# An attention unit's softmax steps re-staged inside the paired MoE blocks

## The chip, the cores and the metric

The kernel runs on one core of a Trainium2 chip. The metric is device time in microseconds (us) of one execution. Its engines are called here as the profile calls them: PE (TensorE, matrix products; PEld is its weight load), DVE (VectorE), ACT (ScalarE), POOL (GpSimd) and SP (SyncE, which here only issues DMAs). Each engine works through its own instructions in the order in which they were written; they wait for each other by semaphores.

## The reference, cut to what is computed

Chunked attention over 64 tokens, then a layer with a hard gate (h times a ramp clipped to 0..1), then a second layer with a softmax, a normalisation and a product. The change touches the attention and the first layer alone.

```python
scores = scale * np.matmul(q_c, k_c.transpose(0, 1, 2, 4, 3))
scores = scores - np.max(scores, axis=-1, keepdims=True)
attn = np.exp(scores)
attn = attn / (np.sum(attn, axis=-1, keepdims=True) + 1e-09)
out = np.matmul(attn, v_c)
...
h = x @ w_in
relu6 = np.clip(h + 3.0, 0.0, 6.0)
g = h * relu6 / 6.0
return (g @ w_out).astype(np.float32)
```

8 heads, 4608 tokens, x of 512, w_in 512x2048, w_out 2048x512, all fp32.

## The kernel before

The 4608 tokens are 36 attention units `u` of 128 tokens and 9 blocks of 512. Blocks 0 to 2 run one at a time, with the attention between their products. Blocks 3 to 8 run as three pairs. Pairs 0 and 1 are `pair_7` (310 to 491 us and 491 to 674 us of the trace); pair 2 is another function, `pair`. The order of all instructions is written out by hand: the scheduler takes them as the code issues them.

A pair computes the two blocks' first layer with seven half-size products in place of eight. **First half** of a pair: eight steps `j` (256 of the 2048 hidden columns each; their results are four quarters, two token blocks by two halves). A step on PE is seven calls of `mul7`, each six matmuls of 128x512 on one PSUM bank: A11 (into bank `a`), S2 (`b`), S1 (`c`), then A22 and S4 *of the step before*, whose banks come in `late` (the function `finish`), then S3 (added to `b`) and A12 (added to `a`). DVE and ACT make four sums of them and gate each: `a` (gated by `gate`, L1230, after a ramp on ACT, L1225), `u3 + c` (L1369, L1371: the quarter `c22`, gated by two ramps on ACT, L1225 and L1227, and a product on POOL, L1374), `s1 + b` after A22 (L1301) and `u2 + c` after S4 (L1305). Four POOL subtractions (`later_sums`, L1318 to L1321) make further operands, and SP stores them. A22 adds to the bank that L1369 has to read first, and S3 to the bank that L1345 has to read first.

In the steps j = 1, 2, 3, 4, 6, 7 an **attention slot** (`att_slot`) stands at the step's end: on PE the scores of unit u+2 and the product of unit u with v, each 32 matmuls of 64x64 (L398). Between them a unit goes through: row maxima (DVE, L410), their scaling by -0.125 (DVE, L431), eight exponentials with sums (ACT, L448), 1/sum (DVE, L454 and L457), the multiplication with it (`attn_norm`, L465; POOL in the first half, DVE in the second), five 32x32-block transposes (`attn_turn`; DVE, L490 and L494), the product with v, and two copies of its result (ACT, L520). In a slot's step of unit u the code issues `attn_norm(u)` and the exponentials of u+1 behind A11, and `attn_turn(u)` behind `finish`. The maxima of u+2 also wait for the two ACT copies, which read the same PSUM tile.

**Second half**: seven products of eight steps (`mul_o`, L1280), whose operands `prepare(d)` splits into a high and a low part (ACT cast L1264, DVE subtraction L1265). `prepare(0)` and `prepare(1)` stand in the last step of the first half, `prepare(2)` behind the last `finish`; the products j = 0, 2, 4, 6 of the second half begin with the operands 0, 1, 2, 3. Two slots stand behind j = 7 of the first and the second product ("slot 0" and "slot 1" below). In pair 1 no unit is left for their scores.

Of the kernel before, what the change touches and what calls it, by code (L numbers as in the profile page):

```python
# [21 lines left out]
def tile_kernel(  # L22
# [404 lines left out]
    def attn_scores_act(u, sc, between=None):  # L427
        mx = maxima(sc)
        if between:
            between()  # L430
        nc.vector.tensor_scalar_mul(out=mx, in0=mx, scalar1=-0.125)  # L431
        exps[u] = sc, mx
# [560 lines left out]
    def att_slot(w, u, coming=None):  # L993
        t = att_psum()
        sc = None
        if u < NU:
            sc = scores(u, t)
        if w is not None:
            if w >= FIRST * UPB:
                attn_pv_raw(w, t, raw_dest(w))  # L1000
            else:
                attn_pv(w, t, *xn[w // UPB])
            p_t.pop(w, None)
        loads = [lambda eng: load_v(w + 2, eng=eng)] if w is not None else []
        if u < NU:
            loads.append(lambda eng: load_qk(u + 1, eng=eng))
        if coming is None:
            for load in loads:
                load(nc.scalar)
        else:  # L1010
            coming.extend(loads)
        if u < NU:
            attn_scores_act(u, sc)

    def raw_dest(w):

# [186 lines left out]
    def o_next():  # L1203
        if pend:
            moe_o(*pend.pop(0))
# [17 lines left out]
    def ramp(h, t, down=False):  # L1223
        s = -1.0 / 6.0 if down else 1.0 / 6.0
        nc.scalar.activation(out=t, in_=h, func=AF.Relu, bias=half_1, scale=s)  # L1225
        if down:
            nc.scalar.activation(out=t, in_=t, func=AF.Relu, bias=one_1, scale=-1.0)  # L1227
# [62 lines left out]
    def pair_7(p, todo):  # L1290
# [5 lines left out]
            while coming:  # L1296
                coming.pop(0)(nc.sync)

        def finish(j, b, c, s1, u2):
            mul7(b, j, "A22", "T4", False, True)  # L1300
            nc.vector.tensor_add(out=b, in0=s1, in1=b)  # L1301
            t = gp_tile("t")
            ramp(b, t)
            mul7(c, j, "S4", "B22", False, True)
            nc.vector.tensor_add(out=c, in0=u2, in1=c)  # L1305
            gate(t, b, g_t["B21", j // 2][:, j % 2])
            t = gp_tile("g_hi")
            ramp(c, t)
            while waiting:
                waiting.pop(0)()  # L1310
            return j, t, c

        def later_sums(j, g12):
# [8 lines left out]
            for i, t in enumerate((t2, t3, t4)):  # L1322
                waiting.append(
                    lambda i=i, t=t: nc.sync.dma_start(out=later_t[i, m][:, k], in_=t)
                )

        event = {1: 0, 2: 1, 3: 2, 4: 3, 6: 4, 7: 5}
        for j in range(NJ):
            u = base + event[j] if j in event else NU
            n = 2 * (j % 2)  # L1330
            a = acc_bank(n) if j else att_psum()[:, 0]
            mul7(a, j, "A11", "B11", True, False)
            s1 = work_tile("s")
            nc.scalar.copy(out=s1, in_=a)
            load_coming()
            while todo:
                todo.pop(0)()
            if base < u < NU:
                attn_norm(u, nc.gpsimd)
                if u + 1 < NU:  # L1340
                    attn_exp_act(u + 1, range(H))
            b = acc_bank(n + 1) if j else h_psum()
            mul7(b, j, "S2", "T2", True, False)
            u2 = work_tile("s")
            nc.vector.tensor_add(out=u2, in0=s1, in1=b)  # L1345
            if j % 2 == 0:
                for g in GROUPS:
                    g_t[g, j // 2] = home(g, j // 2)
            m, k = j // 2, j % 2
            if j == 1:  # L1350
                made = finish(*late)
                mul7(b, j, "S3", "T3", False, False)
            c = h_psum()
            mul7(c, j, "S1", "T1", True, False)
            o_next()
            if j > 1:
                made = finish(*late)
            if base < u < NU:
                attn_turn(u)
            if j == NJ - 1:  # L1360
                prepare(0)
            if made:
                i, t, ps = made
                gate(t, ps, t)
                later_sums(i, t)
            if j != 1:
                mul7(b, j, "S3", "T3", False, False)
            u3 = ap1.tile([P, DM], F32, tag="tx2", name="tx2")
            nc.vector.tensor_add(out=u3, in0=s1, in1=b)  # L1369
            c22 = g_t["B22", m][:, k]  # L1370
            nc.vector.tensor_add(out=c22, in0=u3, in1=c)  # L1371
            t = gp_tile("g_lo")
            ramp(c22, t, True)
            nc.gpsimd.tensor_mul(out=c22, in0=t, in1=c22)  # L1374
            mul7(a, j, "A12", "B21", False, True)
            t = gp_tile("t")
            ramp(a, t)
            o_next()
            if j == NJ - 1:
                prepare(1)  # L1380
            gate(t, a, g_t["B11", m][:, k])
            if u < NU:
                att_slot(u, u + 2, coming)
            late = j, b, c, s1, u2
        i, t, ps = finish(*late)
        gate(t, ps, t)
        prepare(2)
        later_sums(i, t)
# [10 lines left out]
        for i in range(len(OUTS)):  # L1399
# [7 lines left out]
            for j in range(NJ):  # L1407
                mul_o(ps, i, j, i in (0, 1, 3, 6), i in (2, 4, 5, 6))
                d = (i * NJ + j) // 2
                if (i, j) == (0, 5):  # L1410
                    while waiting:
                        waiting.pop(0)()
                if j % 2:
                    bring(d)
                else:
                    prepare(d + 3)
                if (i, j) in steps:
                    todo.pop(0)()
                u = base + 6 + i
                load_coming()  # L1420
                if i < 3:
                    if j == 0 and u < NU:
                        attn_norm(u)
                        if u + 1 < NU:
                            attn_exp_act(u + 1, range(H))
                    elif j == 2 and u < NU:
                        attn_turn(u)
                    elif j == 7 and i < 2:
                        att_slot(u, u + 2, coming)
                if final:  # L1430
                    if (i, j) == (5, 7):
                        second.append(Second())
                    elif (i, j) in ((6, 4), (6, 7)):
                        second[0].window(1, 0, False)
                    if j % 2 and d % 2 == 0 and d > 2 * ND:
                        load_o(d // 2 - ND - 1)
# [198 lines left out]
    for F, n in SLOT_AT.items():  # L1635
        u = 2 * UPB + 1 + n
        STEPS.setdefault(F, []).append(("exp", u, range(H // 2)))
        STEPS.setdefault(F + 1, []).append(("exp", u, range(H // 2, H)))
        if u <= NA:
            STEPS.setdefault(F + 2, []).append(("norm", u, (0, 1, 2)))  # L1640
            STEPS.setdefault(F + 3, []).append(("turn", u, (3, 4)))
    u = 2 * UPB
# [178 lines left out]
```

## Time and profile before

| what | value |
|---|---|
| three runs | median 1222.01 us, 1218.27 to 1223.95 |
| the profiled execution | 1221.51 us, span 1219.7 us |
| busy in the span | PE 97%, PEld 79%, DVE 74%, ACT 59%, POOL 39% |
| granted PE clock, mean | 0.989 |

The span runs from the first to the last instruction; the execution takes 1.8 us more. A row of the timeline says when a group of like instructions started (us from the span's start), how long it took from the start of its first to the end of its last, and in brackets how long its engine had been idle before it and who released it. Matmuls overlap, so a PE row's end is modelled, and the distance between two starts is the better measure. A wait row says who waited for whom, for how long in total, how often, and the longest. The stretch rows give each engine's busy time in it, the granted clock (1.00 is 2.4 GHz, 0.50 is 1.2 GHz), the share of time in which DMA engines were busy, and GB/s.

### The profile page before, as it was taken

The numbers are of one execution on the slowest core, as the hardware profiler recorded it, in microseconds if no ns is written. First come the engines' busy times: TensorE is split into PE (matmuls) and PEld (weight loads), VectorE is DVE, ScalarE is ACT, GpSimd is POOL, SyncE is SP. The second block draws the span as 40 slices with busy tenths as digits, with TensorE's granted clock in tenths as the row PEclk, the third lists the DMA queues.
The fourth block names the chain that finished last, engine by engine and source line by source line (L and its number), as shares of the span: only waits on it lengthen the run. The fifth ranks groups of instructions, "written<-read, shape, count | busy, mean of one in ns | idle before, by whom it ended". The sixth has DMA issues, their size and how long they took to land.

```text
span 1219.7 us, 21402 instructions
## 1 busy us (share of the span) xinstructions
PE 1183.7 (97%) x7199; PEld 960.8 (79%) x7199; DVE 900.8 (74%) x1434; ACT 720.7 (59%) x1655; POOL 479.8 (39%) x560
## 2 busy tenths in 40 slices
PE   8999999999999899999799799999999999999998
PEld 7888877878877688777588688888888888888887
DVE  7888677776577887477867666767987887877774
ACT  7765545554445574345553343355887777777775
POOL 1000674442246400256400011200486758585864
PEclk9999999999999899999899899999999999999999
DMA  9812657765888896788799999882332323232311
GB/s 371 362 52 76 232 209 253 267 234 193 296 296 274 279 390 207 246 283 286 249 330 342 356 348 341 308 311 87 111 96 72 97 70 99 71 98 71 99 55 63
DMA packets 172254, 258.61 MB, mean 212 GB/s; under 512 B 19056, under 2 KB 86896, under 8 KB 172144
## 3 DMA queue, kind: packets, MB, share of 16 engines
q1 hardware_dynamic: 159760, 234.69, 56.5%
q10 hardware_dynamic: 12384, 22.55, 5.3%
q8 instruction: 57, 0.93, 0.3%
q14 instruction: 53, 0.43, 0.1%
HBM read 170.40 MB, written 76.02 MB: 202 GB/s over the span
## 4 chain that ended last, share of the span: by engine, by line
PE 74%; issue 8%; DVE 7%; POOL 5%; ACT 3%; DMA 2%; SPq 0%; POOLq 0%; ACTq 0%; DVEq 0%
PE po L949 16%; PE acc L574 15%; PE hp L535 8%; PE acc L1280 7%; PE b L751 5%; PE hp L1143 5%; PE hp L1280 4%; PE c L751 4%; PE a L751 4%; PE att L1143 2%; PE att L398 2%; PE att L751 1%; DVE wi L1265 1%; DVE pbd L494 1%; PE acc L1143 1%
## 5 line engine op out<-in xcount | busy, mean ns | idle before, releaser
L574 PE MATMUL acc<-g_hi,wo 128*128 128x512 f32 x640 | 164.2, 396 | 0.0
L574 PEld LDWEIGHTS acc<-g_hi,wo 128*128 128x128 f32 x640 | 119.7, 189 | 26.5
L1143 PE MATMUL hp<-wi,w 128*128 128x512 f32 x468 | 119.5, 399 | 7.4 <-ACT wi L319 6.6
L1143 PEld LDWEIGHTS hp<-wi,w 128*128 128x128 f32 x468 | 89.8, 193 | 28.9 <-issue 7.0
L1143 PE MATMUL acc<-wi,w 128*128 128x512 f32 x420 | 106.8, 401 | 3.5 <-DVE tx L1369 3.5
L864 ACT COPY wo<-wo 32x256 f32<-32x256 f32 x228 | 92.1, 404 | 19.4 <-DVE wo L846 11.5
L1280 PE MATMUL acc<-wi,w 128*128 128x512 f32 x408 | 98.0, 398 | 3.3 <-DVE wi L1265 3.0
L535 PE MATMUL hp<-x_hi,wi 128*128 128x512 f32 x384 | 97.8, 396 | 0.1
L1143 PEld LDWEIGHTS acc<-wi,w 128*128 128x128 f32 x420 | 79.3, 191 | 21.4 <-DVE tx L1369 3.8
L1280 PEld LDWEIGHTS acc<-wi,w 128*128 128x128 f32 x408 | 77.3, 191 | 21.9 <-DVE wi L1265 3.8
L732 POOL TENSOR_TENSOR x_lo<-xr,x_hi 128x768 fp32r<-128x768 f32 (+1 forms) x30 | 63.8, 2148 | 75.5 <-ACT x_hi L725 72.6
L448 ACT ACTIVATE p<-att,mx 128x64 f32<-128x64 f32 x256 | 76.5, 322 | 26.5 <-DVE mx L431 18.2
L1265 DVE TENSOR_TENSOR wi<-wo,wi 128x1024 fp32r<-128x1024 f32 x50 | 66.0, 1336 | 32.8 <-ACT wi L1264 32.3
L574 PE MATMUL acc<-g_lo,wo 128*128 128x512 f32 x320 | 87.8, 390 | 0.0
L535 PEld LDWEIGHTS hp<-x_hi,wi 128*128 128x128 f32 x384 | 71.5, 187 | 17.1 <-ACT x_hi L512 0.3
L1264 ACT CAST wi<-wo 128x1024 fp32r<-128x1024 f32 x50 | 51.7, 1070 | 35.8 <-PE hp L1280 19.0
L574 PEld LDWEIGHTS acc<-g_lo,wo 128*128 128x128 f32 x320 | 60.4, 189 | 13.0
L836 DVE SCALAR_TENSOR_TENSOR wo<-wo,r,wo 128x1024 f32<-128x1024 f32 x36 | 68.9, 1913 | 1.3
L933 POOL TENSOR_TENSOR wo<-wo,wo 128x1024 fp32r<-128x1024 f32 x25 | 64.5, 2578 | 6.2 <-ACT wo L929 3.6
L560 POOL TENSOR_TENSOR g_lo<-t,g_hi 128x512 fp32r<-128x512 f32 x15 | 21.5, 1433 | 106.4 <-ACT g_hi L557 106.4
L1454 POOL TENSOR_TENSOR s<-s 128x512 f32<-128x512 f32 x4 | 5.1, 1300 | 130.2 <-DVE s L1453 130.2
L448 ACT ACTIVATION_READ_ACCUMULATOR p<-att,mx 128x1 f32 x256 | 55.0, 215 | 0.0
(318 smaller groups left out, 2873.6 us busy)
## 6 DMA issues: line engine op xcount, KB each, us to landing
w<-sti SPq DMA_DIRECT2D x168, 256.0 KB, 4.7
w<-sto SPq DMA_DIRECT2D x112, 256.0 KB, 4.8
later_t<-xo SPq DMA_DIRECT2D x48, 256.0 KB, 4.7
wo<-later_t SPq DMA_DIRECT2D x24, 512.0 KB, 6.2
wo<-wo SPq DMA_DIRECT2D x328, 32.0 KB, 1.8
x2d<-xo SPq DMA_DIRECT2D x36, 256.0 KB, 4.3
xr<-x2d SPq DMA_DIRECT2D x36, 256.0 KB, 3.3
out<-ob SPq DMA_DIRECT2D x36, 256.0 KB, 2.3
```

Of the source, the lines that this page charges most:

```text
L448: nc.scalar.activation(out=p_t[u][:, h], in_=sc[:, c, a], func=AF.Exp, scale=0.125, bias=mx[:, m : m + 1], accum_out=sums[u][:, h : h + 1],)
L535: nc.tensor.matmul(hp, wi[f][:, a, kk * P : (kk + 1) * P], b[:, kk], start=(n == 0), stop=(n == 3 * KD - 1),)
L574: nc.tensor.matmul(acc[dc], wo[f][:, w, dc * P : (dc + 1) * P], g[i], start=(at == 0 and n == 0), stop=(at == NF - 1 and n == 2),)
L732: eng.tensor_sub(out=lo[:, f], in0=r, in1=hi[:, f].bitcast(F32))
L751: nc.tensor.matmul(ps, x[:, AT[a], j], w2[w, j][i], start=(start and n == 0), stop=(stop and n == 5), skip_group_check=True,)
L836: nc.vector.scalar_tensor_tensor(out=h, in0=e, scalar=r, in1=h, op0=ALU.mult, op1=ALU.mult, accum_out=mu)
L864: move(out=m[b * 32 : b * 32 + 32, a], in_=tr[a * 32 : a * 32 + 32, b])
L933: eng.tensor_sub(out=lo, in0=m, in1=hi.bitcast(F32))
L949: nc.tensor.matmul(po, a[f], out_w[f][w], start=(n == 0), stop=(n == 3 * NF2 - 1),)
L1143: nc.tensor.matmul(ps, w[:, i, kk * P : (kk + 1) * P], x[:, kk], start=(start and n == 0), stop=(stop and n == 5), skip_group_check=True,)
L1265: nc.vector.tensor_sub(out=e[1], in0=src, in1=e[0].bitcast(F32))
L1280: nc.tensor.matmul(ps[s], w[:, k, s * P : (s + 1) * P], x[l], start=(start and j == 0 and n == 0), stop=(stop and j == NJ - 1 and n == 2), ...
```

## The change

Four things move, all in the pairs' attention and in `pair_7`:

1. **The quarter c22 is gated one step later** (`gate_22`): its two ramps on ACT and its product on POOL are issued behind A11 and its copy in the next step, not behind S3.
2. **The maxima are scaled by ACT** (`nc.scalar.mul` in `stage("exp")`), right ahead of the exponentials, not by DVE (14 units).
3. **A unit is normalised in the step of its exponentials and turned first thing in the next.** `stage` issues: in the step of unit u the transposes of u and the exponentials of u+1 behind A11, and 1/sum of u+1 inside `finish`, between A22 and S4. The multiplication is on POOL everywhere; five of them were on DVE, in the second halves. There the transposes and exponentials stand at j = 0 and 1/sum at j = 2.
4. **The slot at a step's end stands ahead of `prepare(1)` and of the gating of `a`**, so that the maxima go first on DVE.

PE's and SP's instructions are the same and in the same order. DVE has 19 fewer (14 scalings, 5 multiplications), ACT 14 more, POOL 5 more.

```diff
+            exps[u] = sc, maxima(sc)
+            due["exp"].add(u)
...
+        if what == "exp":
+            nc.scalar.mul(out=exps[u][1], in_=exps[u][1], mul=-0.125)
+            attn_exp_act(u, range(H))
+            due["norm"].add(u)
+        elif what == "norm":
+            attn_norm(u, nc.gpsimd)
+            due["turn"].add(u)
+        else:
+            attn_turn(u)
...
-        def finish(j, b, c, s1, u2):
+        def finish(j, b, c, s1, u2, between):
             mul7(b, j, "A22", "T4", False, True)
             nc.vector.tensor_add(out=b, in0=s1, in1=b)
             t = gp_tile("t")
             ramp(b, t)
+            between()
             mul7(c, j, "S4", "B22", False, True)
...
-            if base < u < NU:
-                attn_norm(u, nc.gpsimd)
-                if u + 1 < NU:
-                    attn_exp_act(u + 1, range(H))
+            if late:
+                gate_22(late[0])
+            stage("turn", u)
+            stage("exp", u + 1)
...
-                made = finish(*late)
-            if base < u < NU:
-                attn_turn(u)
+                made = finish(*late, lambda: stage("norm", u + 1))
...
-            t = gp_tile("g_lo")
-            ramp(c22, t, True)
-            nc.gpsimd.tensor_mul(out=c22, in0=t, in1=c22)
             mul7(a, j, "A12", "B21", False, True)
             t = gp_tile("t")
             ramp(a, t)
             o_next()
+            if u < NU:
+                att_slot(u, u + 2, coming)
             if j == NJ - 1:
                 prepare(1)
             gate(t, a, g_t["B11", m][:, k])
-            if u < NU:
-                att_slot(u, u + 2, coming)
...
                 if i < 3:
-                    if j == 0 and u < NU:
-                        attn_norm(u)
-                        if u + 1 < NU:
-                            attn_exp_act(u + 1, range(H))
-                    elif j == 2 and u < NU:
-                        attn_turn(u)
+                    if j == 0:
+                        stage("turn", u)
+                        stage("exp", u + 1)
+                    elif j == 2:
+                        stage("norm", u + 1)
```

How the instructions stand. DVE in a step with a slot, pair 0, before (`mx` maxima, `sm` sums, `p` exponentials, `pbd` transposed; `hp` and `acc` are the PSUM banks, `tx` is u3, `wo` the gated quarters):

```order
L1305 TENSOR_TENSOR hp<-s,hp 128x512
L1230 SCALAR_TENSOR_TENSOR wo_3791<-t,acc_3862 128x512
L490 STREAM_TRANSPOSE pbd<-p 128x512
L494 STREAM_TRANSPOSE pbd<-p 32x8x32 x4
L1230 SCALAR_TENSOR_TENSOR g_hi<-g_hi,hp 128x512
L1369 TENSOR_TENSOR tx_4079<-s,acc_4008 128x512
L1371 TENSOR_TENSOR wo_4021<-tx_4079,hp 128x512
L1230 SCALAR_TENSOR_TENSOR wo_4019<-t,acc_3979 128x512
L410 TENSOR_REDUCE mx<-att 128x8
L431 TENSOR_SCALAR mx<-mx 128x8
L454 TENSOR_SCALAR sm<-sm 128x8
L457 RECIPROCAL sm<-sm 128x8
```

The same place after (L1327, L1251, L1395, L1397 and L1373 are the lines L1305, L1230, L1369, L1371 and L1345 of before):

```order
L454 TENSOR_SCALAR sm<-sm 128x8
L457 RECIPROCAL sm<-sm 128x8
L1327 TENSOR_TENSOR hp<-s,hp 128x512
L1251 SCALAR_TENSOR_TENSOR wo_3791<-t,acc_3862 128x512
L1251 SCALAR_TENSOR_TENSOR g_hi<-g_hi,hp 128x512
L1395 TENSOR_TENSOR tx_4082<-s,acc_4013 128x512
L1397 TENSOR_TENSOR wo_4026<-tx_4082,hp 128x512
L410 TENSOR_REDUCE mx<-att 128x8
L1251 SCALAR_TENSOR_TENSOR wo_4024<-t,acc_3977 128x512
L490 STREAM_TRANSPOSE pbd<-p 128x512
L494 STREAM_TRANSPOSE pbd<-p 32x8x32 x4
L1373 TENSOR_TENSOR s<-s,acc_4013 128x512
```

The transposes left the place between the two gates for the start of the next step, the scaling L431 is gone, and 1/sum stands ahead of the sum that waits for S4.

ACT in the same step, before (`g_lo` is the ramp of c22, `t` and `g_hi` those of the other quarters):

```order
L448 ACTIVATE p,sm<-att,mx 128x64 x8
L1225 ACTIVATE t<-acc_3862,three 128x512
L1225 ACTIVATE g_hi<-hp,three 128x512
L1225 ACTIVATE g_lo<-wo_4021,three 128x512
L1227 ACTIVATE g_lo<-g_lo,three 128x512
L1225 ACTIVATE t<-acc_3979,three 128x512
L520 COPY xr_3956<-att 128x2x2x64
L520 COPY wi_3957<-att 128x2x2x64
L1334 COPY s<-acc_4135 128x512
```

And after:

```order
L1027 ACTIVATE mx<-mx 128x8
L448 ACTIVATE p,sm<-att,mx 128x64 x8
L1246 ACTIVATE t<-acc_3862,three 128x512
L1246 ACTIVATE g_hi<-hp,three 128x512
L1246 ACTIVATE t<-acc_3977,three 128x512
L520 COPY xr_3954<-att 128x2x2x64
L520 COPY wi_3955<-att 128x2x2x64
L1362 COPY s<-acc_4133 128x512
L1246 ACTIVATE g_lo<-wo_4026,three 128x512
L1248 ACTIVATE g_lo<-g_lo,three 128x512
```

The two ramps of c22 moved behind the copy that opens the next step, and the scaling of the maxima came in ahead of the exponentials.

DVE where the first half of pair 0 ends, before (`wi` are the operands that `prepare` makes):

```order
L490 STREAM_TRANSPOSE pbd<-p 128x512
L494 STREAM_TRANSPOSE pbd<-p 32x8x32 x4
L1265 TENSOR_TENSOR wi_4773<-wo_3788,wi_4772 128x1024
L1230 SCALAR_TENSOR_TENSOR g_hi<-g_hi,hp 128x512
L1369 TENSOR_TENSOR tx_4792<-s,acc_4721 128x512
L1371 TENSOR_TENSOR wo_4576<-tx_4792,hp 128x512
L1265 TENSOR_TENSOR wi_4810<-wo_4019,wi_4809 128x1024
L1230 SCALAR_TENSOR_TENSOR wo_4574<-t,acc_4692 128x512
L410 TENSOR_REDUCE mx<-att 128x8
```

And after:

```order
L1286 TENSOR_TENSOR wi_4776<-wo_3788,wi_4775 128x1024
L1251 SCALAR_TENSOR_TENSOR g_hi<-g_hi,hp 128x512
L1395 TENSOR_TENSOR tx_4795<-s,acc_4726 128x512
L1397 TENSOR_TENSOR wo_4581<-tx_4795,hp 128x512
L410 TENSOR_REDUCE mx<-att 128x8
L1286 TENSOR_TENSOR wi_4846<-wo_4024,wi_4845 128x1024
L1251 SCALAR_TENSOR_TENSOR wo_4579<-t,acc_4690 128x512
```

The transposes are no longer ahead of the first `prepare` subtraction, and the maxima stand ahead of the second.

## Rows read from the trace of the kernel before

**Rows 1.** The page, part 1: busy time, share of the span, instructions.

```profile
PE 1183.7 (97%) x7199; PEld 960.8 (79%) x7199; DVE 900.8 (74%) x1434; ACT 720.7 (59%) x1655; POOL 479.8 (39%) x560
```

**Rows 2.** Waits of PE: engine line <- releaser: us in total, times, longest.

```profile
PE att L398 <- DVE pbd L494: 11.4, 20, 2.8
PE hp L1143 <- ACT wi L319: 6.6, 1, 6.6
```

**Rows 3.** Timeline of PE, pair 0: slots of steps 1 to 3, and what follows.

```profile
329.39 0.69 PE L398 MATMUL att<-kbd,q 64*64 64x64 f32 x32
...
330.48 3.02 PE L1143 MATMUL acc<-wi,w 128*128 128x512 f32 x12
...
340.30 0.69 PE L398 MATMUL att<-kbd,q 64*64 64x64 f32 x32
...
342.08 3.04 PE L1143 MATMUL acc<-wi,w 128*128 128x512 f32 x12
...
351.92 0.69 PE L398 MATMUL att<-kbd,q 64*64 64x64 f32 x32
...
354.54 3.03 PE L1143 MATMUL acc<-wi,w 128*128 128x512 f32 x12
```

**Rows 4.** Timeline of PE, pair 0: last step of the first half to slot 0.

```profile
388.20 3.04 PE L1143 MATMUL acc<-wi,w 128*128 128x512 f32 x12
...
402.49 2.93 PE L1143 MATMUL acc<-wi,w 128*128 128x512 f32 x6 [1.77 <-DVE tx L1369]
...
414.85 6.92 PE L1280 MATMUL acc<-wi,w 128*128 128x512 f32 x22 [1.49 <-DVE wi L1265]
...
424.21 11.29 PE L1280 MATMUL hp<-wi,w 128*128 128x512 f32 x48
```

**Rows 5.** Timeline of PE, pair 1: the same place.

```profile
568.29 3.03 PE L1143 MATMUL acc<-wi,w 128*128 128x512 f32 x12
...
604.77 13.77 PE L1280 MATMUL hp<-wi,w 128*128 128x512 f32 x48
```

**Rows 6.** Stretches: PE, PEld, DVE, ACT, POOL busy, clock, DMA share, GB/s.

```profile
402.00:404.00 2.00, 1.51 (x4) 1.22 (x5) 1.12 (x2) 0.77 (x2) 1.92 (x2) 0.50 0.15 53
606.00:608.00 2.00, 2.00 (x6) 1.52 (x6) 0.58 (x2) 2.00 (x4) 0.00 (x0) 0.50 0.31 126
```

**Rows 7.** Timeline of ACT and DVE, pair 0, the step from 342.08.

```profile
345.75 0.38 ACT L520 COPY wi<-att 128x256 f32<-128x256 f32 x1
...
346.95 0.59 DVE L431 TENSOR_SCALAR mx<-mx 128x8 f32<-128x8 f32 x1
...
347.64 0.32 ACT L448 ACTIVATE p<-att,mx 128x64 f32<-128x64 f32 x1 [1.03 <-DVE sm L454]
...
349.97 0.72 ACT L1225 ACTIVATE t<-acc,three 128x512 f32<-128x512 f32 x1
...
350.73 0.69 DVE L1230 SCALAR_TENSOR_TENSOR wo<-t,acc 128x512 f32<-128x512 f32 x1 [0.75 <-DMA w<-sti]
...
352.07 1.80 DVE L494 STREAM_TRANSPOSE pbd<-p 32x256 f32<-32x256 f32 x4
```

**Rows 8.** Timeline of DVE, second half of pair 0: maxima behind slot 1.

```profile
437.33 0.69 DVE L410 TENSOR_REDUCE mx<-att 128x8 f32<-128x512 f32 x1 [1.02 <-ACT wi L520]
```

**Rows 9.** POOL beside DVE: timeline rows, and durations (ns, min/median/max) of L490.

```profile
380.46 1.30 POOL L1321 TENSOR_TENSOR xo<-wo,xo 128x512 f32<-128x512 f32 x1
380.48 1.30 DVE L454 TENSOR_SCALAR sm<-sm 128x8 f32<-128x8 f32 x1
406.22 2.03 DVE L1265 TENSOR_TENSOR wi<-wo,wi 128x1024 fp32r<-128x1024 f32 x1 [3.06 <-ACT wi L1264]
L490 DVE STREAM_TRANSPOSE pbd<-p x29: 696/706/714, 97.6 to 610.8; 128x512 f32<-128x512 f32 x29
```

**Rows 10.** Timeline, pair 0, last step of the first half: the first `prepare`.

```profile
397.22 1.10 ACT L1264 CAST wi<-wo 128x1024 fp32r<-128x1024 f32 x1
...
400.02 1.23 DVE L1265 TENSOR_TENSOR wi<-wo,wi 128x1024 fp32r<-128x1024 f32 x1
```

More of the change, by code (lines that the diff above doesn't have):

```diff
@@ L1011, in att_slot, with stage @@
             coming.extend(loads)
-        if u < NU:
+        if u >= NU:
+            return
+        if coming is None:
             attn_scores_act(u, sc)
+        else:
+            exps[u] = sc, maxima(sc)
+            due["exp"].add(u)
+    due = {n: set() for n in ("exp", "norm", "turn")}
+    def stage(what, u):
+        if u not in due[what]:
+            return
+        due[what].remove(u)
+        if what == "exp":
[5 more added lines that the diff above has]
+            due["turn"].add(u)
+        else:
+            attn_turn(u)
     def raw_dest(w):
@@ L1325, in later_sums, with gate_22 @@
                 )
+        def gate_22(j):
+            h = g_t["B22", j // 2][:, j % 2]
+            t = gp_tile("g_lo")
+            ramp(h, t, True)
+            nc.gpsimd.tensor_mul(out=h, in0=t, in1=h)
         event = {1: 0, 2: 1, 3: 2, 4: 3, 6: 4, 7: 5}
@@ L1356, in pair_7 @@
             if j > 1:
-                made = finish(*late)
-            if base < u < NU:
-                attn_turn(u)
+                made = finish(*late, lambda: stage("norm", u + 1))
             if j == NJ - 1:
@@ L1381, in pair_7 @@
             gate(t, a, g_t["B11", m][:, k])
-            if u < NU:
-                att_slot(u, u + 2, coming)
             late = j, b, c, s1, u2
-        i, t, ps = finish(*late)
+        gate_22(NJ - 1)
+        i, t, ps = finish(*late, lambda: None)
         gate(t, ps, t)
@@ L1638, in tile_kernel @@
         STEPS.setdefault(F + 1, []).append(("exp", u, range(H // 2, H)))
-        if u <= NA:
+        if u > NA:
+            due["norm"].add(u)
+        else:
             STEPS.setdefault(F + 2, []).append(("norm", u, (0, 1, 2)))
```

## The prediction

> **What bounds the kernel now.** I read the page first: PE is busy for 97% of the span [rows 1], so what can be won is PE's idle time and the time at half clock. The list of PE's waits says where that idle time lies: 11.4 us in 20 waits of the product with v for the transposes, and 6.6 us in one wait at the entry of the last pair, which the change doesn't touch [rows 2]. The timeline of PE then tells what a slot costs. One that waits for nothing takes 330.48 − 329.39 = 1.09 us, that of step 2 takes 1.78 and that of step 3 takes 2.62 [rows 3]. Seven products take 340.30 − 330.48 = 9.82 us, 1.40 each [rows 3]; so a step with a slot can be done in 10.91 us.
>
> Why are the transposes late? In the step from 342.08 the exponentials wait 1.03 us for DVE, run from 347.64 to 349.97, and only then ACT does the ramp on which DVE's gate of 350.73 waits (its row names a DMA, but the ramp ended at 350.69, just ahead of it); the transposes are queued behind that gate and end at 353.87 [rows 7], while the scores are through by 352.6 [rows 3]. DVE has nothing to do meanwhile; it stands in the wrong place of its queue.
>
> The worst place is the end of a first half. From A11 of the last step to the end of slot 0 pair 0 takes 424.21 − 388.20 = 36.01 us [rows 4]. Its work is 7 + 2 + 8 products and two slots: 17 x 1.40 + 2 x 1.09 = 26.0. So 10.0 us are lost: the late transposes, a wait of 1.77 us for L1369, one of 1.49 us for the third `prepare` subtraction, and half clock behind the first of them, 0.50 granted from 402 to 404 [rows 4, 6]. Pair 1 takes 604.77 − 568.29 = 36.48 us [rows 5] for 25.5 (no scores in slot 0): 11.0 lost. There the clock was still at 0.50 behind it [rows 6], so that the next 48 matmuls took 13.77 where pair 0 took 11.29 [rows 4, 5]: 2.5 more.
>
> **The steps with a slot.** The clock of a step starts with A11; products are 1.40 us apart, S3 begins at 7.0, the scores at 9.8, the step ends at 10.9. Work it through for the new order.
> - DVE: the maxima come first and wait for both ACT copies of the slot's result, as the maxima behind slot 1 do (1.02 us [rows 8]); copies behind the end of the v product put them at some 1.0 (an estimate: two copies like the 0.38 of [rows 7] and a handover). Then maxima 0.7, gate 0.7, transposes 0.7 + 1.8, the sum L1345 0.7: done at 5.6. S3 needs it at 7.0. Margin 1.4.
> - ACT: the copy of A11 at 2.3, two ramps of 0.72 to 3.7, the scaling, eight exponentials of 2.33 together [rows 7]. No ACT operation of 128x8 is in the trace; its price lies between 0 (the 0.59 that DVE gives back for it is the larger) and the 0.32 of a 128x64 exponential [rows 7]; I take 0.3. The exponentials end at 6.4.
> - The new wait: L454 stands on DVE until then. Queued behind it are the sum after S4, two gates and the two sums of the next quarter. S4 ends at 7.0, so the sum after it could not have started before 7.2: the wait costs nothing. It would cost once the exponentials ended past 6.8.
> - Then 7.2 + 5 x 0.7 = 10.7: the last sum of the step is through before the next maxima could start at 11.9. DVE keeps some 1.2 us of slack in each step, ACT and POOL more (POOL: six operations of at most 1.30 [rows 9], 7.8 of 10.9).
> - The product with v at 10.3 meets transposes that ended at 4.9.
>
> So a slot falls to 1.09. Steps 2, 3, 4, 6 of a pair (3 and 4 alike, 2 and 6 alike): 2 x 0.69 + 2 x 1.53 = 4.4; two pairs, **8.9 us**. The other edits come to nothing here: c22's later gate ends on POOL around 5, and the subtractions that use it start at 9.4; the 14 scalings of 0.59 and less come off a DVE that waits anyway; PE's and SP's orders are the same, and SP's stores find their subtractions done at 3.7 of a step, ahead of the 7.0 at which SP comes to them.
>
> **The end of a first half.** Same zero, A11 of the last step. The ramp behind S4 ends at 8.6, the cast of `prepare(0)` takes 1.10, its subtraction 1.23 [rows 10]: 10.9. Behind it on DVE stand a gate and L1369, 12.3; A22 needs L1369, and the slot ends at 10.9. So PE still waits, some 1.35 us, where it lost about 1.5 in the slot (as in step 3) and then waited 1.77. The subtraction of `prepare(1)` follows the maxima and ends at 14.9, or at 15.7 if POOL's subtractions stand in its way as in the row of 2.03 [rows 9]; PE asks for it past 17.7. That of `prepare(2)` ends between 20.6 and 21.6; PE asks for it at 20.5, or at 21.9 if the clock fell. Transposes for slot 0 follow the fourth subtraction and end by 26.3; slot 0 comes at 27. Half clock followed the wait of 1.77 [rows 4, 6]; 1.35 is nearer to that than to no wait, so I take it again: six matmuls of 2.93 us in place of 1.54, 1.4. (Without it the wait for `prepare(2)` costs about as much.) Sum: 26.0 + 1.35 + 1.4 = 28.7 for 36.0, a gain of 7.3. Pair 1: 28.2 for 36.5, and no half clock behind slot 0: 8.3 + 2.5 = 10.8. Together **18.1 us**.
>
> **The second halves.** Five multiplications of 128x512 move from DVE to POOL, which is idle there, and 1/sum waits for exponentials two products earlier in the same half. `prepare` runs three operands (8 us of PE) ahead, so what DVE loses there stays off PE. What POOL does to DVE shows in the rows: a 128x8 operation of DVE took 1.30 us while a POOL operation of 1.30 ran, and a `prepare` subtraction 2.03 where it took 1.23 alone; transposes take 696 to 714 ns in all 29 cases, whatever POOL does [rows 9, 10]. The Trainium skill, SBUF — State Buffer (section "SBUF: two separate sides"), says that VectorE and GpSimd share one port pair as an exclusive lock, held for a whole instruction, against VectorE operations with two SBUF inputs or in a two-port mode. It speaks against this edit, and the rows agree: each of the five could hold a subtraction for one POOL operation, some 1 us. By the rule alone that would be 5 us on DVE; on PE it is 0 with the lead of 8 us, and at most 5 without it.
>
> **The sum.** 8.9 + 18.1 = 27.0 us off. The profiled execution took 1221.5 (span 1219.7), 0.5 under the median of the runs; from the median, 1222.0 − 27.0 = **1195.0**.
>
> **Rivals.**
> - *The end of the first half stays as it is* (0.17). DVE's queue there is long, POOL's subtractions hold its `prepare` subtractions, and the clock falls. For it: the 2.03 row, and that both casts stand behind ACT's other work. Against it: 2.5 us of transposes leave this place. Gain: the 8.9 of the steps alone, 1213. The page named above bears on it: an exclusive lock would hold DVE just here.
> - *Pair 1's gain is given back* (0.08). The entry to the last pair waits 6.6 us for weights [rows 2]; if those arrive at their own time, PE waits longer for them. Their loads are issued behind PE's own progress, which speaks against it. 1222 − 4.4 − 7.3 = 1210.
> - *The transposes come no earlier* (0.06). They need POOL's multiplication, which stands behind c22's product; if POOL ran a step late, the slots would wait as before: 1222. By the count above POOL has 3 us of slack.
> - *Slower* (0.05). A loop through three engines: c22 → its two ramps (1.45) → scaling (0.3) → exponentials (2.4) → 1/sum (0.5) → sum after S4, two gates, two sums (3.5) = 8.2 us, now in series in each step. From 10.9 on it sets the step, so it takes 2.7 us of handovers that I don't see. At 12.9 the ten steps with a slot would stand 0.8 over their present mean (10.91 + 1.19 = 12.1), and the ends would win nothing: 1222 + 8 = 1230.
>
> My forecast has the rest, 0.64.
>
> **How the numbers follow.** Nothing lost at all would be 8.9 + 10.0 + 11.0 + 2.5 = 32.4 off: 1189.6, the lower end. Upwards the range takes in the first two rivals: 1213. Outside remain the last two and a little, under 0.2. A measurement of this kernel tells 0.5%, 6.1 us, from no change. Faster by that: 0.64 + 0.17 + 0.08 = 0.89, less a little for small sums: 0.87; within it 0.07; slower 0.06.
>
> **What would show it.** Right: PE's waits for L494 vanish; slots of about 1.1 us in all steps; L454 behind the exponentials, and the sum after S4 still waiting for PE and not for L454; A11 of the last step to the end of slot 0 in some 28.7 us; a wait for L1369's successor of 1 to 1.5 us left. Wrong: slots still near 2.6 us; S3 or A22 waiting for DVE inside a step (the loop); waits for `prepare` subtractions in the second half; a longer wait than 6.6 us at the last pair's entry.

## The result, and the profile after

The changed kernel takes 1193.03 us, median of four runs (1192.38 to 1193.68); the kernel before, beside it on the same chip, 1220.79 (1218.27 to 1223.95). The ratio is 0.9771, with a 95% interval of 0.9746 to 0.9797. The profiled execution took 1193.68, its span 1192.0; that of before was 1219.7, so 27.7 us lie between the two traces. One execution, of e5 below, took 2995.64 us, with 829 ns for a 128x512 matmul that takes 393 in that kernel's other trace and with a granted clock of 1.00 throughout; its cause is open, and no number here uses it.

The page, part 1, and what PE waits for (us in total, times, longest), as [rows 1, 2] before:

```profile
PE 1169.7 (98%) x7199; PEld 952.9 (80%) x7199; DVE 890.2 (75%) x1415; ACT 727.9 (61%) x1669; POOL 491.5 (41%) x565
```

```profile
PE hp L1164 <- ACT wi L319: 6.3, 1, 6.3
...
PE acc L1164 <- DVE tx L1395: 2.2, 2, 1.1
...
PE att L398 <- DMA kbd<-in_k: 1.5, 1, 1.5
```

The 20 waits of the product with v for the transposes [rows 2] are gone. One wait for the sum of c22 is left in each pair, and one wait for k has come.

PE's timeline, pair 0: a step with its slot, then the last step of the first half to both slots of the second, as [rows 3, 4] before.

```profile
341.01 0.69 PE L398 MATMUL att<-kbd,q 64*64 64x64 f32 x32
...
342.10 3.02 PE L1164 MATMUL acc<-wi,w 128*128 128x512 f32 x12
...
384.46 3.02 PE L1164 MATMUL acc<-wi,w 128*128 128x512 f32 x12
...
396.56 1.66 PE L1164 MATMUL acc<-wi,w 128*128 128x512 f32 x6 [1.12 <-DVE tx L1395]
...
411.60 11.28 PE L1301 MATMUL hp<-wi,w 128*128 128x512 f32 x48
424.38 0.69 PE L398 MATMUL att<-kbd,q 64*64 64x64 f32 x32 [1.50 <-DMA kbd<-in_k]
```

Pair 1, the end of the first half and the first product behind slot 0, as [rows 5]:

```profile
552.80 3.02 PE L1164 MATMUL acc<-wi,w 128*128 128x512 f32 x12
...
579.47 11.26 PE L1301 MATMUL hp<-wi,w 128*128 128x512 f32 x48
590.67 0.69 PE L398 MATMUL att<-pbd,v 64*64 64x64 f32 x32
```

A slot takes 342.10 − 341.01 = 1.09 us, and so does every slot inside a first half. From A11 of the last step to the end of slot 0 it is 411.60 − 384.46 = 27.14 us in pair 0 (36.01 before) and 579.47 − 552.80 = 26.67 in pair 1 (36.48). The 48 matmuls behind it take 590.67 − 579.47 = 11.20 in pair 1 (13.71 from start to start before).

Where the 27.7 us went: eight slots 2 x 4.45 = 8.9, the two ends 8.9 and 9.8, the half clock behind pair 1's slot 0 2.5: 30.1 won. Given back: 1.5 for the wait for k, and 0.7 ahead of the first slot of pair 0. That leaves 27.9. The 0.7 isn't the change's: the first slot of pair 0 started anywhere from 329.0 to 330.8 in the traces of all kernels here.

Part of what was won is clock. Before, half clock was granted behind the wait for c22's sum in pair 0 [rows 6] and in pair 1 (0.50 from 584 to 586 us), behind pair 1's slot 0 [rows 6], and once more in pair 0, behind the 1.49 us for L1265 [rows 4], which the prediction did not list:

```profile
416.00:418.00 2.00, 2.00 (x6) 1.52 (x6) 2.00 (x2) 2.00 (x3) 2.00 (x1) 0.50 1.02 406
```

Those 22 matmuls took 421.70 − 414.85 = 6.85 us from start to start; the same 22 took 416.42 − 411.18 = 5.24 in e2, at 1.00. Reckoned in this way all four stretches cost some 7 us (1.3, 1.6, 1.6 and 2.5; an estimate), a quarter of the gain. After the change 1.00 was granted at all four places.

### The profile page after: what moved, and what is told of

Its sections match the earlier page's. It is cut to its first block, busy times and chain, and to the rows that moved or that the text cites. A ratio compares the mean times of both kernels' runs of the same rounds, so it can differ in the third digit from the quotient of the medians.

```text
span 1192.0 us, 21417 instructions
## 1 busy us (share of the span) xinstructions
PE 1169.7 (98%) x7199; PEld 952.9 (80%) x7199; DVE 890.2 (75%) x1415; ACT 727.9 (61%) x1669; POOL 491.5 (41%) x565
## 4 chain that ended last, share of the span: by engine, by line
PE 91%; DVE 3%; DMA 2%; POOL 1%; ACT 1%; issue 1%; SPq 1%; ACTq 0%; POOLq 0%; DVEq 0%
PE acc L574 17%; PE po L949 16%; PE hp L535 9%; PE acc L1301 9%; PE hp L1164 9%; PE acc L1164 8%; PE b L751 6%; PE c L751 4%; PE a L751 4%; PE hp L1301 3%; PE att L398 3%; PE att L1164 2%; PE att L751 1%; POOL xo L1090 1%; DMA xr<-in_moe_w_in 1%
## 5 line engine op out<-in xcount | busy, mean ns | idle before, releaser
L1164 PEld LDWEIGHTS hp<-wi,w 128*128 128x128 f32 x468 | 89.2, 191 | 28.2 <-issue 6.7
L1164 PE MATMUL acc<-wi,w 128*128 128x512 f32 x420 | 104.4, 395 | 2.2 <-DVE tx L1395 2.2
L1301 PE MATMUL acc<-wi,w 128*128 128x512 f32 x408 | 95.3, 392 | 0.0
L1286 DVE TENSOR_TENSOR wi<-wo,wi 128x1024 fp32r<-128x1024 f32 x50 | 66.2, 1344 | 24.1 <-ACT wi L1285 23.6
L1285 ACT CAST wi<-wo 128x1024 fp32r<-128x1024 f32 x50 | 51.4, 1065 | 33.4 <-PE hp L1301 16.6
L828 ACT ACTIVATE wo<-wo,nmx 128x1024 f32<-128x1024 f32 x36 | 41.5, 1152 | 22.4 <-DVE nmx L825 22.3
L541 ACT ACTIVATE t<-hp,three 128x512 f32<-128x512 f32 x48 | 33.3, 694 | 35.0 <-PE hp L535 32.4
```

Source lines behind the costliest of these rows:

```text
L1164: nc.tensor.matmul(ps, w[:, i, kk * P : (kk + 1) * P], x[:, kk], start=(start and n == 0), stop=(stop and n == 5), skip_group_check=True,)
L1286: nc.vector.tensor_sub(out=e[1], in0=src, in1=e[0].bitcast(F32))
L1301: nc.tensor.matmul(ps[s], w[:, k, s * P : (s + 1) * P], x[l], start=(start and j == 0 and n == 0), stop=(stop and j == NJ - 1 and n == 2), ...
```

## Experiments

All in one table first. "Steps" is pair 0 from the end of step 1's slot to A11 of the last step; "end" is from there to the end of slot 0. Times in us, from each trace; the ratio is to the kernel before, which was run beside each of them (medians there 1220.8 to 1223.2).

| kernel | steps | end, pair 0 | end, pair 1 | median | ratio, 95% interval |
|---|---|---|---|---|---|
| before | 57.7 | 36.0 | 36.5 | 1222.0 | 1 |
| changed | 53.3 | 27.1 | 26.7 | 1193.0 | 0.9771 (0.9746–0.9797) |
| e1 scaling on DVE | 53.3 | 27.2 | 26.7 | 1195.6 | 0.9777 (0.9762–0.9792) |
| e3 slot last | 53.3 | 27.2 | 26.7 | 1195.1 | 0.9775 (0.9759–0.9791) |
| e9 multiplications on DVE | 53.3 | 27.2 | 26.7 | 1193.7 | 0.9775 (0.9760–0.9790) |
| e2 c22 in its own step | 54.5 | 31.1 | 30.6 | 1205.3 | 0.9853 (0.9838–0.9867) |
| e4 transposes late | 56.0 | 30.1 | 28.0 | 1203.1 | 0.9840 (0.9823–0.9856) |
| e11 third item undone, multiplication still on POOL | 56.0 | 33.1 | 33.1 | 1211.8 | 0.9911 (0.9886–0.9935) |
| e5 third item alone | 54.0 | 33.4 | 32.9 | 1206.9; again 1205.5 | 0.9878 (0.9852–0.9903); 0.9872 |
| e7 2.2 us more on DVE | 55.6 | 28.8 | 28.8 | 1201.5 | 0.9841 (0.9824–0.9857) |
| e8 longer wait | 53.3 | 29.5 | 27.4 | 1197.1 | 0.9796 (0.9774–0.9817) |
| e10 still longer wait | 53.3 | 29.9 | 28.1 | 1198.9 | 0.9818 (0.9803–0.9832) |
| e6 two waits removed | 53.3 | 26.0 | 25.5 | 1191.1 | 0.9748 (0.9728–0.9768) |

My theory was that the time went with the place of the transposes. Its rivals were that another of the four items carries the gain: the scaling, c22's deferral or the slot's place.

### The scaling and the slot's place, undone one at a time

e1:

```diff
-            exps[u] = sc, maxima(sc)
+            attn_scores_act(u, sc)
...
-            nc.scalar.mul(out=exps[u][1], in_=exps[u][1], mul=-0.125)
```

> The change, with the maxima scaled by VectorE again, right behind the maxima. Theory (the time went with the place of the transposes; DVE has 1 us of slack in a step): DVE gets 0.6 us per unit back, the transposes end at 5.1 of a step and not 4.5, the sum that S3 waits for at 5.9 of 7.0, so 1193 us, within 1.5. Rival (the scaling carries the gain, DVE sets the steps): slots longer by up to 0.6 us in ten steps and more at the ends of the first halves, 1199 to 1205.

e3:

```diff
-            if u < NU:
-                att_slot(u, u + 2, coming)
             if j == NJ - 1:
                 prepare(1)
             gate(t, a, g_t["B11", m][:, k])
+            if u < NU:
+                att_slot(u, u + 2, coming)
```

> The change, with the slot behind prepare(1) and the gating of a again. Theory: in a step DVE waits about 1 us for the slot's copies anyway, and the gate fits in there; at the end of a first half the subtraction of prepare(1) stands ahead of the maxima, which nobody waits for soon: 1193 us, within 1.5. Rival (the maxima ahead of the gate matter): maxima 0.7 us later in each step, the exponentials with them, 1198 or more.

Both are the changed kernel again, 0.9777 and 0.9775. In e1 DVE had more to do than I thought, since the scaling ran beside a POOL operation (1.00 us in place of 0.59). DVE's timeline in a step of e1 (start, us):

```profile
343.77 1.00 DVE L431 TENSOR_SCALAR mx<-mx 128x8 f32<-128x8 f32 x1
...
347.83 0.69 DVE L1372 TENSOR_TENSOR s<-s,acc 128x512 f32<-128x512 f32 x1
```

The sum for S3 ends 6.3 us after A11 (342.22) in place of 5.3, and S3 asks for it at 7.0. So it shows nowhere.

### c22 gated in its own step (e2)

```diff
-            if late:
-                gate_22(late[0])
...
             nc.vector.tensor_add(out=c22, in0=u3, in1=c)
+            gate_22(j)
...
-        gate_22(NJ - 1)
```

> The change, with c22 gated in its own step again. Theory A (only the place of the transposes counts): 1193 us, within 2. Theory B (the two ramps of c22, 1.45 us on ScalarE ahead of the ramp of a and of the two copies of the slot's result, hold these copies and so the maxima until 2.9 of a step; the transposes behind them end at 6.8, the sum at 7.5, and S3 waits some 0.5 to 0.8 us in each of ten steps): 1198 to 1203, with waits of S3 for L1373 in the trace. Rival C (this part carries most of the gain): above 1210.

Slower than the changed kernel by 0.0082 of 1222, 10 us: near theory B's 5 to 10, and my "only the transposes" falls. But the place is another than theory B said. The steps lose only 1.3 us in pair 0. The ends lose 3.9 each. PE waits in e2, and ACT's and DVE's timeline at the end of the first half of pair 0:

```profile
PE acc L1301 <- DVE wi L1286: 3.0, 2, 1.5
...
PE acc L1301 <- ACT wi L1285: 1.7, 2, 0.8
...
PE acc L1164 <- DVE s L1371: 1.5, 5, 0.3
```

```profile
400.32 0.73 ACT L1246 ACTIVATE g_lo<-wo,three 128x512 f32<-128x512 f32 x1 [3.27 <-POOL wo L1340]
...
402.95 0.69 DVE L410 TENSOR_REDUCE mx<-att 128x8 f32<-128x512 f32 x1 [2.72 <-ACT wi L520]
...
408.92 4.43 DVE L1286 TENSOR_TENSOR wi<-wo,wi 128x1024 fp32r<-128x1024 f32 x2 [0.25 <-ACT wi L1285]
```

ACT cannot begin c22's ramps before DVE has made c22 (L1395, done at 400.23; the row names a POOL operation that was done at 400.27, so which of the two came last is not shown), and the ramp of `a`, the slot's copies and the cast of `prepare(1)` stand behind them. ACT stood still until 400.32, the maxima waited 2.72 us for the copies, and the casts and subtractions that the second half asks for came so late that PE waited for them. The fence's last row is the subtractions of `prepare(2)` and `prepare(3)`; their casts started at 407.85.

### The transposes late (e4), the whole third item undone (e11), and alone (e5)

e4 moves `stage("turn", u)` behind `finish`, e11 also `stage("norm", u)` into the step of unit u:

```diff
-            stage("turn", u)
             stage("exp", u + 1)
...
                 made = finish(*late, lambda: stage("norm", u + 1))
+            stage("turn", u)
             if j == NJ - 1:
                 prepare(0)
```

> The change, with only the transposes put back behind finish in the first halves (1/sum stays a step ahead). Theory (the place of the transposes carries the gain): they start behind two gates at 8.6 of a step and end at 11.1, the product with v is due at 10.3, so the slots take 1.9 to 2.6 us, ten times 0.8 to 1.5 us more, and each end of a first half loses 3 to 8 us again: 1207 to 1223. Rival (the earlier 1/sum, the scaling or the deferred c22 carry it): slots stay under 1.4 us, 1199 or less.

> The change without its third item: a unit is normalised and turned in its own slot's step, as before; c22 later, scaling by ScalarE and the slot's place stay. Theory (after the run with the transposes behind finish, in which each slot still took 1.77 us): the deferred c22 and the scaling free the exponentials, ramps and gates, the transposes end at the same 0.4 us too late, and the earlier 1/sum gives nothing more: 1202 to 1205, slots of 1.77 in all steps. Rival (without the earlier 1/sum the other items give nothing, as I had read the trace of before): 1215 to 1222, slots of up to 2.6.

e4 costs 8.4 us (0.0069), under my range and above the rival's. Every slot of a first half from step 2 on takes 1.77 us there, none 2.6, and so it is in e11. PE's timeline in e4: the slot of step 3 and the A11 behind it, then the A22 behind the slot of step 7, which lost the same 0.7 us before its wait:

```profile
351.79 0.69 PE L398 MATMUL att<-kbd,q 64*64 64x64 f32 x32
...
352.95 0.68 PE L398 MATMUL att<-pbd,v 64*64 64x64 f32 x28 [0.36 <-DVE pbd L494]
353.56 3.04 PE L1164 MATMUL acc<-wi,w 128*128 128x512 f32 x12
...
399.86 1.90 PE L1164 MATMUL acc<-wi,w 128*128 128x512 f32 x6 [1.77 <-DVE tx L1395]
```

In e11 slot 0 of the second half is lost besides: its multiplication stands on POOL behind four subtractions of `later_sums`. DVE and PE in e11:

```profile
416.47 0.71 DVE L490 STREAM_TRANSPOSE pbd<-p 128x512 f32<-128x512 f32 x1 [2.17 <-POOL p L465]
...
418.15 0.33 PE L398 MATMUL att<-pbd,v 64*64 64x64 f32 x4 [3.03 <-DVE pbd L494]
```

So 1/sum a step ahead has a worth of its own, 8.7 us (0.9911 − 0.9840), nearly all where the first half ends. My expectation for e11 held in the steps and missed this. It is also the place where e11 differs from the kernel before, which had this multiplication on DVE. So the 8.7 us hold with the multiplication on POOL alone; with it on DVE, as before, the late 1/sum may cost less, and that was not run.

e5 is the kernel before with the third item alone (e1, e2 and e3 together), run a second time for its trace.

> The kernel before with the third item alone (normalised with the exponentials, turned first thing in the next step); c22 is gated in its own step, VectorE scales the maxima and the slot stands last. Theory (the parts overlap: c22's ramps hold the slot's copies as in the run with c22 alone undone, and the scaling now adds 0.6 us to the chain that ends in the sum for S3): 1.0 to 1.3 us wait in each of some eight steps and the same waits at the ends as there, 1206 to 1212. Rival (the third item carries nothing by itself): 1218 or more. Rival (it carries all): 1195 or less.

> The kernel before with the third item alone, once more for its trace. Theory (c22's ramps and the scaling on VectorE delay the sum that S3 waits for): about 1208 us, with waits of S3 of 0.8 to 1.2 us for L1371 in most steps with a slot, none of the product with v for the transposes in them. Rival (the transposes still come late): waits of the product with v for L494 in the steps.

Near the theory's time, 1206.9 and 1205.5, but again not by waits in most steps: S3 waited three times.

```profile
PE acc L1300 <- ACT wi L1284: 3.3, 2, 1.6
...
PE acc L1163 <- DVE s L1370: 1.1, 3, 0.4
```

The loss is at the ends once more, by the route of e2, and some 2.9 us of it are clock: behind these waits 0.50 was granted in both pairs, and 22 matmuls took 6.70 and 6.65 us there for the 5.24 of e2. The third item undone costs 17 us (e11, with the reservation above), the three others 12 to 13 (e5): together 29 to 30, against the 28 that the change brings. The two are nearly additive, and neither is idle.

### How much of DVE's time was free (e7)

The large transpose is done four times:

```diff
-            attn_turn(u)
+            attn_turn(u, [0] * 3 + list(range(5)))
```

> The change, with the large transpose done four times in place of once: 3 x 0.70 = 2.1 us more on VectorE per unit. Theory (in the changed kernel the sum ends at 5.3 of a step and S3 asks for it at 7.0, so 1.7 us of VectorE's time there are free): S3 waits for L1373, 0.4 to 0.6 us in each of ten steps, and the ends of the first halves lose 0 to 2 us each; 1197 to 1202. Rival (the queue of VectorE sets the steps already): 2.1 us in each of ten steps, 1214. Rival (nothing reaches TensorE): 1193 to 1195.

DVE's and PE's timeline, e7:

```profile
343.80 2.94 DVE L490 STREAM_TRANSPOSE pbd<-p 128x512 f32<-128x512 f32 x4
```

```profile
341.78 3.02 PE L1164 MATMUL acc<-wi,w 128*128 128x512 f32 x12
...
349.33 3.02 PE L1164 MATMUL acc<-wi,w 128*128 128x512 f32 x12 [0.41 <-DVE s L1373]
...
353.38 3.02 PE L1164 MATMUL acc<-wi,w 128*128 128x512 f32 x12
```

2.94 − 0.70 = 2.24 us more on DVE make the step 353.38 − 341.78 = 11.60 long, 0.69 more than 10.91. So 1.55 us were free at this place of the queue, where I had counted a margin of 1.4. A wait of 0.41 in a row costs 0.69 from start to start.

### The clock behind the wait for c22's sum (e8, e10)

One more subtraction of 128x512 behind `prepare(0)` in e8, two in e10:

```diff
             if j == NJ - 1:
                 prepare(0)
+                src, (hi, lo) = g_t[HOMES[0], 0], parts_o[0, 0]
+                for _ in range(1):
+                    nc.vector.tensor_sub(
+                        out=lo, in0=src[:, 0], in1=hi.bitcast(F32)
+                    )
```

> The change, with one more subtraction of 128x512 on VectorE in the last step of a first half (half of the first prepare's subtraction, done twice), so that TensorE's wait for L1395 grows from 1.12 us to about 1.75, as long as in the kernel before. Theory (half clock follows this wait once it is as long as there): the granted clock falls to 0.50 behind it, 1.4 us more per pair, and the sum is 1196 to 1198. Rival (the clock did not follow that wait but the row of waits before and behind it): 1194 to 1195, no stretch of half clock there.

> The change, with two more subtractions of 128x512 on VectorE in the last step of a first half, so that TensorE's wait for L1395 grows from 1.12 us to about 2.5 (1.85 with one more, where the clock fell in pair 0 and not in pair 1). Theory (the longer the wait, the surer the fall of the clock): half clock behind it in both pairs, 1.4 us or more each; 1193 + 2 x 1.4 + 2 x 1.4 = 1198 to 1200. Rival (the clock's fall does not go by the length of this wait): at most one of the two pairs at half clock, 1195.5 to 1198.

In both the clock fell in pair 0 and not in pair 1. PE's timeline of e10, pair 0 and pair 1, and the stretches behind the waits (columns as in [rows 6]):

```profile
397.26 2.93 PE L1164 MATMUL acc<-wi,w 128*128 128x512 f32 x6 [2.57 <-DVE tx L1400]
...
568.39 1.66 PE L1164 MATMUL acc<-wi,w 128*128 128x512 f32 x6 [2.57 <-DVE tx L1400]
```

```profile
397.00:399.00 2.00, 1.74 (x4) 1.45 (x5) 1.97 (x4) 0.95 (x2) 1.92 (x2) 0.50 0.19 64
569.00:571.00 2.00, 2.00 (x10) 1.65 (x9) 2.00 (x3) 1.45 (x2) 1.84 (x3) 1.00 0.04 16
```

The times are those of the theory, 1197.1 and 1198.9, but the clock fell in one pair and not in both: there e10's rival was right, though its range ended at 1198. The same wait, in the same place, is followed by half clock or not. Over the kernels here, behind the wait for c22's sum (pair 0, pair 1):

| wait, us | kernels | clock fell |
|---|---|---|
| 1.12 | changed, e1, e3, e9 | never |
| 1.54 to 1.56 | e2, e5, e7 | never |
| 1.77 | before; e4; e11 | both; pair 0; neither |
| 1.84, 1.85 | e8 | pair 0 |
| 2.57 | e10 | pair 0 |

The table holds for this wait alone. Elsewhere the clock fell behind shorter ones: behind 1.49 us in the kernel before (416 to 418 us, above), and at both ends of e5, where 1.6 us for L1284 and 1.50 for L1285 follow each other with two matmuls between them. In e2 0.8 and 1.50 us at the same place left it at 1.00. The clock also changes from one execution of a kernel to the next: e3 took 1193.71 us at a mean granted clock of 0.996 and 1197.48 at 0.991, e1 1194.14 at 0.996 and 1196.76 at 0.992 (the last one is the trace, with 0.50 behind a wait of 2.0 us for k). The length of the wait alone does not decide it; what does stays open.

### The multiplications of the second halves on DVE (e9)

```diff
-                        stage("norm", u + 1)
+                        stage("norm", u + 1, nc.vector)
```

> The change, with the multiplications of the second halves on VectorE again, as before. Theory (neither engine is asked for there): 1193 us, within 1.5, no new wait of TensorE. Rival (the port that VectorE and GpSimd share made the multiplications on GpSimd cost): faster by up to 5 us, 1188 to 1191. Rival (on VectorE they push the prepare subtractions back): 1195 to 1198, with waits for L1286 in the second halves.

No difference: 0.9775 against 0.9771. The same place of both kernels, first the changed one, then e9 (DVE and POOL):

```profile
411.79 3.17 DVE L1286 TENSOR_TENSOR wi<-wo,wi 128x1024 fp32r<-128x1024 f32 x2
412.02 1.86 POOL L465 TENSOR_TENSOR p<-p,sm 128x512 f32<-128x512 f32 x1 [0.41 <-DVE sm L457]
```

```profile
411.69 0.69 DVE L465 TENSOR_TENSOR p<-p,sm 128x512 f32<-128x512 f32 x1
412.30 2.35 DVE L1286 TENSOR_TENSOR wi<-wo,wi 128x1024 fp32r<-128x1024 f32 x2
```

On POOL the multiplication takes 1.86 us where it takes 1.04 alone, and DVE's two subtractions beside it 3.17 where they take 2.35 alone: 0.82 lost on DVE for 0.69 saved. The Trainium skill, SBUF — State Buffer (section "SBUF: two separate sides"), describes a lock by which one of the two engines blocks the other for a whole instruction. The rows agree with it, and the move relieved nobody. On PE it is nothing either way.

### Two of the waits that are left (e6)

```diff
-            if j == NJ - 1:
-                prepare(0)
...
             nc.vector.tensor_add(out=c22, in0=u3, in1=c)
+            if j == NJ - 1:
+                prepare(0)
...
-            coming.extend(loads)
+            coming.extend(loads[::-1])
```

> The change, with two waits of TensorE taken away: in the last step of a first half the first prepare stands behind both sums of c22, and a slot's loads of the next q and k are issued ahead of its v. Theory: the wait of 1.12 us for L1395 in each of two pairs goes, and most of the 1.50 us wait for k behind the first second-half product: 1189 to 1191, in any case 2 to 4 us below the changed kernel. Rival (they are given back at the entry of the last pair, which waits for weights that come at their own time): 1193, with the wait there longer by what was won.

PE's timeline of e6, and its waits:

```profile
384.33 3.02 PE L1164 MATMUL acc<-wi,w 128*128 128x512 f32 x12
...
395.24 1.66 PE L1164 MATMUL acc<-wi,w 128*128 128x512 f32 x6
...
410.29 11.26 PE L1301 MATMUL hp<-wi,w 128*128 128x512 f32 x48
```

```profile
PE att L398 <- DMA kbd<-in_k: 0.8, 1, 0.8
```

The wait for L1395 is gone, and the end takes 410.29 − 384.33 = 25.96 us, the 26.0 of bare work. The wait for k fell only from 1.5 to 0.8, less than I expected of it, and the wait at the last pair's entry (L319) is with 7.2 us 0.9 longer than in the changed kernel's trace; it was between 6.3 and 8.0 in the kernels here, so that some of the gain may be given back there. The median is 1191.12 (1190.64 to 1192.20), all four runs below the changed kernel's four. But its ratio of 0.9748 (0.9728 to 0.9768) overlaps that of the changed kernel: the ends are shown to be shorter, by 1.2 us each, and the whole time likely so.

## Why the prediction was right, point by point

1195.0 was forecast and 1193.0 measured; 27.0 us off in the sum, 27.7 between the two traces. The sum is nearer than its terms, and that is luck: the ends won 3.1 us more than forecast, and 2.2 us that the forecast did not have went the other way.

- **The steps: right.** 8.9 us, all slots 1.09. The step worked through on paper is the step of the trace: DVE, ACT and POOL after, A11 at 342.10, as [rows 7] before:

```profile
342.92 0.69 DVE L410 TENSOR_REDUCE mx<-att 128x8 f32<-128x512 f32 x1 [1.09 <-ACT wi L520]
...
345.67 0.19 ACT L1027 ACTIVATE mx<-mx 128x8 f32<-128x8 f32 x1
...
346.68 0.69 DVE L1373 TENSOR_TENSOR s<-s,acc 128x512 f32<-128x512 f32 x1
...
348.52 0.16 DVE L454 TENSOR_SCALAR sm<-sm 128x8 f32<-128x8 f32 x1
...
349.28 0.70 DVE L1327 TENSOR_TENSOR hp<-s,hp 128x512 f32<-128x512 f32 x1 [0.37 <-PE hp L1164]
...
352.12 0.69 DVE L1397 TENSOR_TENSOR wo<-tx,hp 128x512 f32<-128x512 f32 x1
```

  Maxima at 0.8 (forecast 1.0), the sum for S3 done at 5.3 (5.6), the exponentials at 6.1 (6.4), the last sum at 10.7 (10.7), the scaling 0.19 us (0.3). L454 started at 6.4, held by the sum ahead of it (L1322) and no longer by the exponentials, and L1327 waits for PE, not for L454: the new wait costs nothing.
- **The ends: mechanism right, one term too many.** Forecast 26.0 + 1.35 + 1.4 = 28.7 and 28.2; measured 27.14 and 26.67. The wait for c22's sum was 1.12 (1.35 forecast), and the half clock behind it did not come: 1.00 was granted in both pairs, and behind pair 1's slot 0 too, where the kernel before had 0.50 at the same places (two of them in [rows 6]).

```profile
397.00:399.00 2.00, 2.00 (x11) 1.61 (x10) 2.00 (x3) 1.56 (x3) 1.84 (x3) 1.00 0.64 210
565.00:567.00 2.00, 2.00 (x9) 1.66 (x10) 2.00 (x3) 1.75 (x3) 1.92 (x2) 1.00 0.83 294
580.00:582.00 2.00, 2.00 (x10) 1.62 (x9) 1.99 (x3) 2.00 (x4) 1.64 (x1) 1.00 0.99 378
```

  I had put as much on the other case, that without half clock the wait for `prepare(2)` costs the 1.4 us. That was wrong as well. PE has no wait for L1286 in the changed kernel: the subtraction of `prepare(2)` ended at 404.53, 20.1 of the step in place of 20.6 to 21.6, and PE came to it at 20.5 (halfway through the 48 matmuls from 399.43 to 410.51).

```profile
403.30 1.23 DVE L1286 TENSOR_TENSOR wi<-wo,wi 128x1024 fp32r<-128x1024 f32 x1 [0.25 <-ACT wi L1285]
```

  I took the half clock for a property of such a wait, from one row. e8, e10 and the table of waits show it as something that may or may not follow. This mis-sized term, 1.4 us in each pair, is 2.8 us of the 3.1 by which the gains of 27.0 became 30.1.
- **Pair 1's clock behind slot 0: right,** 2.5 us.
- **The wait for k: not foreseen,** 1.5 us the other way. I had called SP's order unchanged, and left it at that. SP's queue in the kernel before, then in the changed one, and what SP waited for there from 412 to 419 us:

```profile
427.42 0.43 SPq L130 DMA_DIRECT2D kbd<-in_k  x1
```

```profile
417.01 0.32 SPq L1295 DMA_DIRECT2D wo<-later_t  x1
...
418.80 0.43 SPq L130 DMA_DIRECT2D kbd<-in_k  x1
```

```profile
SPq L1295 <- DMA later_t<-xo: 2.5, 1, 2.5
```

  SP stood until 417.01 for a load of `bring`, with the load of k behind it: issued 8.3 us after slot 0's scores began (410.51), where it was 5.7 before (427.42 after 421.70). The order is the same, but the load of `bring` reads what a store ahead of it in SP's queue writes, and SP stood 2.5 us until that store had landed. In the kernel before SP waited for PE there (2.4 and 2.3 us) and only 0.5 for such a store. PE now arrives earlier; the store, which follows POOL's subtractions, does not come earlier by as much: it had gone out 1.0 us ahead of slot 0's scores before, and goes out 1.4 us behind them now. e1, e3, e9 and e10 have the wait for k too (1.3 to 2.0), e4, e6, e7 and e8 a shorter one (0.5 to 0.8), e2, e5 and e11, with their longer first halves, none.
- **"The other edits come to nothing here": true of two, wrong of one.** The scaling and the slot's place are worth nothing measurable (e1, e3). c22's deferral I priced only as an edit that costs nothing. It is a condition of the gain: without it 10 us come back (e2), since c22's two ramps would hold ACT for everything behind them. The sum came out right because I had worked the step through with c22 moved; the attribution to the transposes' place alone, with which I began the experiments, did not hold.
- **The second halves: right,** 0 on PE, and e9 the same. But POOL was not idle there, as I had put it: its last subtraction ended 0.41 us before the multiplication of slot 0's unit (e9's first rows), and in e11 the multiplication stood behind it. The rivals did not come: no slot waits for L494, and the three-engine loop has 1.55 us left at the place that I loaded (e7). The rival of a gain given back at the last pair's entry didn't come with the change itself, 6.3 us for 6.6 [rows 2].

## What to carry to other kernels

Work one period of the loop through on paper for every engine, in its own order, and write down when each result is there and when it is asked for: in the step these times were right to 0.3 us, and the 8.9 us with them. An edit that costs nothing may still be what makes another one pay; before giving the gain to one of them, ask what the queue would look like without each. And of a clock that fell once behind a wait, take the cost as a chance between nothing and that row, not as a term.

## What the runs showed of the hardware that was not expected

- Half clock (1.2 GHz) behind a wait of PE is not fixed by the wait. Behind the wait for c22's sum it came after 2.57 us in pair 0 and not in pair 1, after 1.77 us in three of six cases, after 1.56 us and less in none of 14; but after 1.49 us at another wait of the kernel before. The Trainium skill, TensorE: Matmul & The Clock Gate (Part 1), says that the window in which the chip watches TensorE is free-running, not started by the kernel, and that the point of a clock change varies for that reason. That the place of a wait in it decides here would fit the rows; no run here shows it.
- ACT scales a 128x8 tile in 0.19 us, where the trace of before had only allowed me bounds of 0 and 0.32. The Trainium skill, ScalarE: Activation LUTs (section "What ACT_TABLE_LOAD costs"), gives 186 ns + 0.833 ns times N for an ACTIVATE on a [128, N] tile with immediate scale and bias; for N = 8 that is an estimate of 0.19 us, and the row agrees.
